# Sixty-two maxima instead of forty-eight between the q projections, and a new split of the x and q tiles in the first stage

## The chip, the cores and the metric

One Trainium2 chip, of which one core is used. The metric is the device time of one execution in microseconds (us); lower is better. The kernel before takes 1730.11 us, the median of three runs (1729.96, 1730.11 and 1730.19).

## The reference

The input `x` has 2048 rows (the sequence) and 640 columns. Two things are computed from it and mixed by a gate, all in float32:

```python
g = _sigmoid((x * gate_w).sum(-1, keepdims=True))
# A: real part of a Fourier transform along both axes, as matrix products
a = x @ dft_hid_re.T ; b = x @ dft_hid_im.T
y = dft_seq_re @ a - dft_seq_im @ b
# B: attention with 32 heads of 20 columns that share one k and one v
q = (x @ wq) ; k = x @ wk ; v = x @ wv            # q: 32 heads x 20
p = softmax(q_h @ k.T * 20 ** -0.5) ; o_h = p @ v
out = g * y + (1 - g) * (concat(o_h) @ wo)
```

The softmax needs the maximum of each row of scores. This kernel computes the scores twice: once only for the maxima ("a" matmuls, each followed by a maximum on VectorE), and a second time, with the maximum already in the contraction, for the exponential ("b" matmuls).

## The kernel before, in words

**Number format.** A float32 product is made of three products of rounded parts: each operand is split into a high part (rounded, tagged float32r) and the low rest, and `mm3` adds high x high, high x low and low x high in PSUM. A split is one copy on ScalarE (the high part) and one subtraction on VectorE (the low part); weights and later tiles are split on GpSimd.

**Stages.** The program runs in four parts.

1. *The q stage.* The sequence is cut in four blocks of 512 columns (ROW); the contraction over 640 is cut in five chunks of 128. For each block n there is a `kv` product of 10 matmuls (k, v and the gate together), four small transposes `kvt`, and five q projections (m = 0 to 4) of 15 matmuls each. `q_out` reads a finished projection from PSUM, splits it into the tiles `qh` and `ql`, and stores both to DRAM (`qh_d`, `ql_d`). `load_qs0` and `load_qs` read rows of one head pair back into `qs`, in the layout that the scores need. `kv_out` writes k into the tile `ks` by six small moves per block.
2. *Between the projections,* from block 1 on, some of the maxima of head pair 0 are computed: `a_half` issues one score matmul of 60 rows and 512 columns on TensorE and one `tensor_reduce` on VectorE that takes its maximum. The table `slots` says after which projections, and four calls are made each time, into the PSUM banks S1, S2, S3 and S4. Before the change that is 2 x 4 in block 1, and 5 x 4 in each of blocks 2 and 3: 48.
3. *The lead stage.* The first 8 groups of the Fourier part (`ab`, 120 steps of two matmuls with 64 rows and 320 columns each) run with further maxima between them, until 2 x (32 + 12) = 88 maxima are done in all: 40 in this stage before the change. The banks of these maxima are S2, S3 and S4 in turn; the groups of `ab` use S0 with F0 and S1 with F1, in turn.
4. *The loop,* and then a tail, which hold most of the time: the rest of the Fourier part, maxima, exponentials and their products with v, by hand-written plans. The change touches none of it.

**What sets the order.** On TensorE, ScalarE, VectorE and GpSimd the instructions stand in the order of the code. All moves go through one queue on SyncE (SP in the profile), and that queue is ordered by the framework's scheduler, not by the code: it may put a load ahead of moves that stand earlier in the code. SP issues strictly one after the other: a move that waits holds up all behind it.

**Tiles and banks that the change touches.** `xr` holds a block of x (five chunks) until it is split, with two buffers; `qh` and `ql` have three buffers each, and each is free again when its store to DRAM has landed. The eight PSUM banks are S0 to S4, F0, F1 and V; in blocks 1 to 3 the banks F1, V, S0 and F0 are handed out in turn to `kv`, `kvt` and the q projections. Two buffers named raw (`raw_tile`) are shared by parts of `wq`, the weights of the Fourier part (`load_w`, loaded as two parts and split on GpSimd by `split_w`), and the first tiles of x for the lead stage (`load_x`, the loads `xraw` that the first `ab` groups read).

Of the kernel before, what the change touches and what calls it, by code (L numbers as in the profile page):

```python
# [8 lines left out]
F32 = mybir.dt.float32  # L9
F32R = mybir.dt.float32r  # L10
AF = mybir.ActivationFunctionType
ALU = mybir.AluOpType
# [5 lines left out]
P = 128  # L18
S = 2048
# [3 lines left out]
KC = D // P  # L23
# [6 lines left out]
ROW = 512  # L30
# [3 lines left out]
def kernel(  # L34
# [13 lines left out]
    nc = tc.nc  # L48
# [64 lines left out]
    def move(dst, src):  # L113
        nc.sync.dma_start(words(dst), words(src))  # L114
# [22 lines left out]
    xT_v = xT.rearrange("(c p) t -> p c t", p=P)  # L137
# [167 lines left out]
    def a_half(hh, tag="A"):  # L305
        u = state[hh]
        if u >= NA:
            return
        a_unit(u, hh, tag)
        if steps:  # L310
            f, v = steps.pop(0)
            f(v)
        state[hh] = u + 1
        if state[1 - hh] <= u:
            return
        v, r = divmod(u, UV)
        if r == 8 and v + 1 < 2 * NPAIR:
            load_qs(v + 1)
        if r == UV - 1:
            steps.extend((f, v) for f in (a_reduce, a_turn, a_high, a_final))  # L320
            if not stage["loop"]:
                do_chores()
# [24 lines left out]
    with ExitStack() as c1:  # L347
        w1 = c1.enter_context(tc.tile_pool(name="w1", bufs=1, side="right"))
        x1 = c1.enter_context(tc.tile_pool(name="x1", bufs=2, side="right"))
        rot = Rot(["S1", "S0", "F0", "S2", "S3", "S4", "F1", "V", "S0", "F0"])  # L350
        kvg = w1.tile([P, KC, 41], F32, name="kvg")
        kvgs = w1.tile([P, KC, P], F32R, name="kvgs")
        nc.gpsimd.memset(kvgs.bitcast(F32), 0.0)
        nc.gpsimd.memset(ks.bitcast(F32), 1.0)
        nc.gpsimd.memset(vsb, 1.0)
        wqh = w1.tile([P, KC, D], F32R, name="wqh")
        wql = w1.tile([P, KC, D], F32R, name="wql")
        wq_v = wq.rearrange("(c p) n -> p c n", p=P)
        xs, xsp = {}, {}

        def load_x1(n, c):
            if n < 4:
                if c == 0:
                    xs[n] = x1.tile([P, KC, ROW], F32, name="xr")
                move(xs[n][:, c], xT_v[:, c, n * ROW : (n + 1) * ROW])

        def split_x1(n, c):
            if n < 4:
                if c == 0:
                    xh = x1.tile([P, KC, ROW], F32R, name="xh")  # L370
                    xl = x1.tile([P, KC, ROW], F32R, name="xl")
                    xsp[n] = (xh, xl)
                xh, xl = xsp[n]
                nc.scalar.activation(xh[:, c], xs[n][:, c], AF.Copy)
                nc.vector.tensor_tensor(xl[:, c], xs[n][:, c], xh[:, c].bitcast(F32), op=ALU.subtract)

        def q_mm(ps, n, m, c):
            ms = slice(m * P, (m + 1) * P)
            xh, xl = xsp[n]
            mm3(ps, wqh[:, c, ms], wql[:, c, ms], xh[:, c], xl[:, c], KC, c)  # L380

        def q_out(ps, n, m):
            ms, ts = slice(m * P, (m + 1) * P), slice(n * ROW, (n + 1) * ROW)
            qh = x1.tile([P, ROW], F32R, name="qh", bufs=3)
            ql = x1.tile([P, ROW], F32R, name="ql", bufs=3)
            nc.scalar.activation(qh, ps, AF.Copy)
            nc.vector.tensor_tensor(ql, ps, qh.bitcast(F32), op=ALU.subtract)
            move(qh_d[ms, ts], qh)
            move(ql_d[ms, ts], ql)

        def kv_mm(ps, n, c):
            xh, xl = xsp[n]
            end = c == KC - 1
            for high in (not end, end):
                m, x = (105, xh) if high else (41, xl)
                nc.tensor.matmul(ps[:m], kvgs[:, c, :m], x[:, c], start=(c == 0 and high), stop=(end and high))

        def kv_out(ps, n):
            ts = slice(n * ROW, (n + 1) * ROW)
            kvT = x1.tile([41, ROW], F32, name="kvT")  # L400
            kvl = x1.tile([41, ROW], F32, name="kvl", bufs=1)
            kh = x1.tile([DH, ROW], F32R, name="kh")
            kl = x1.tile([DH, ROW], F32R, name="kl")
            nc.scalar.activation(kvl, ps[64:105], AF.Copy)
            nc.vector.tensor_tensor(kvT, ps[:41], kvl, op=ALU.add)
            nc.scalar.activation(kh, kvT[:DH], AF.Copy)
            nc.vector.tensor_tensor(kl, kvT[:DH], kh.bitcast(F32), op=ALU.subtract)
            for r0 in (0, 64):
                move(ks[r0 : r0 + 20, ts], kh)
                move(ks[r0 + 20 : r0 + 40, ts], kl)  # L410
                move(ks[r0 + 40 : r0 + 60, ts], kh)
            return kvT

        def kv_turn(kvT, n, rot):
            ps = rot(f"kvt_{n}")
            for j in range(4):
                nc.tensor.transpose(
                    ps[:, 64 * j : 64 * j + 41], kvT[:, j * P : (j + 1) * P], ident[:41, :41]
                )
            pv = ps.rearrange("p (j c) -> p j c", c=64)[:, :4]  # L420
            ns = slice(4 * n, 4 * n + 4)
            nc.scalar.activation(vsb[:, ns, :DH], pv[:, :, DH : 2 * DH], AF.Copy)
            nc.vector.tensor_copy(
                gz[:, ns].rearrange("p (j o) -> p j o", o=1), pv[:, :, 2 * DH : 2 * DH + 1]
            )


        def gate_out():
            nc.vector.tensor_scalar_max(gz, gz, -87.0)
            nc.scalar.activation(omg, gz, AF.Exp, scale=-1.0)  # L430
            nc.vector.tensor_scalar_add(omg, omg, 1.0)
            nc.vector.reciprocal(gate, omg)
            nc.vector.tensor_scalar(omg, gate, -1.0, 1.0, op0=ALU.mult, op1=ALU.add)

        load_x1(0, 0)
        move(kvg, wkvg.rearrange("(c p) n -> p c n", p=P))
        pkv = rot("kv_0")
        pq = [rot(f"q_0_{m}") for m in range(KC)]
        for c in range(KC):
            if c:  # L440
                load_x1(0, c)
            raw = raw_tile([P, D], "wraw") if c in (2, 3) else w1.tile([P, D], F32, name="wraw", bufs=2)
            move(raw, wq_v[:, c])
            if c == 0:
                nc.vector.tensor_copy(kvgs[:, :, :41], kvg)
                nc.vector.tensor_tensor(
                    kvgs[:, :, 64:105], kvg, kvgs[:, :, :41].bitcast(F32), op=ALU.subtract
                )
            split_x1(0, c)
            split(raw, wqh[:, c], wql[:, c])  # L450
            kv_mm(pkv, 0, c)
            for m in range(KC):
                q_mm(pq[m], 0, m, c)
        for c in range(KC):
            load_x1(1, c)
        for c in range(KC):
            split_x1(1, c)
        kvT = kv_out(pkv, 0)
        for m in range(KC):
            q_out(pq[m], 0, m)  # L460
        load_qs0(0)
        rot = Rot(["F1", "V", "S0", "F0"])
        slots = {1: (2, 3), 2: range(KC), 3: range(KC)}
        for n in range(1, 4):
            for c in range(KC):
                load_x1(n + 1, c)
            pkv = rot(f"kv_{n}")
            for c in range(KC):
                kv_mm(pkv, n, c)
            kv_turn(kvT, n - 1, rot)  # L470
            kvT = kv_out(pkv, n)
            if n == 3:
                for k in range(2):
                    load_x(k)
            for m in range(KC):
                ps = rot(f"q_{n}_{m}")
                for c in range(KC):
                    q_mm(ps, n, m, c)
                split_x1(n + 1, m)
                q_out(ps, n, m)  # L480
                if (n, m) == (1, 0):
                    load_qs0(1)
                if m in slots[n]:
                    for z in range(4):
                        a_half(z % 2, f"S{1 + z}")
                if (n, m) == (3, 1):
                    kv_turn(kvT, 3, rot)
                    gate_out()
                if n == 3 and m in (2, 3):
                    split_x(m - 2)  # L490
                if (n, m) == (3, 3):
                    load_x(2)
            if n < 3:
                load_w(n - 1, 0)
                split_w(n - 1)
# [102 lines left out]
    op = ctx.enter_context(tc.tile_pool(name="op", bufs=2))  # L598
# [605 lines left out]
```

## Time and profile before

| What | us |
|---|---|
| Median of the three runs | 1730.11 |
| The profiled execution, its time | 1732.34 |
| The profiled execution, span of its instructions | 1730.6 |
| q stage: first matmul of a `kv` product to the last of the last projection | 6.0 to 102.4 |
| Lead stage: first `ab` matmul to the first `b` matmul | 102.9 to 130.4 |
| Loop and tail | 130.4 to 1730.6 |

The profile is one execution, taken by the hardware. Its page gives busy times and a chain of work that ended last; the timeline, read for one engine or for all, gives the start and the length of each instruction, what its engine waited for before it (in brackets, with the releaser), and how many instructions were merged in the row (x). PE is TensorE, DVE is VectorE, ACT is ScalarE, POOL is GpSimd, SPq is the queue that issues the moves. A row of the windows view gives, for a stretch of time, the busy us of PE, PE's weight loads, DVE, ACT and POOL, each with its count of instructions, then the granted TensorE clock as a share of full speed, the share of DMA time and GB/s.

### The profile page before, as it was taken

The numbers are of one execution on the slowest core, as the hardware profiler recorded it, in microseconds if no ns is written. First come the engines' busy times: TensorE is split into PE (matmuls) and PEld (weight loads), VectorE is DVE, ScalarE is ACT, GpSimd is POOL, SyncE is SP. The second block draws the span as 40 slices with busy tenths as digits, with TensorE's granted clock in tenths as the row PEclk, the third lists the DMA queues.
The fourth block names the chain that finished last, engine by engine and source line by source line (L and its number), as shares of the span: only waits on it lengthen the run. The fifth ranks groups of instructions, "written<-read, shape, count | busy, mean of one in ns | idle before, by whom it ended". The sixth has DMA issues, their size and how long they took to land.

```text
span 1730.6 us, 43337 instructions
## 1 busy us (share of the span) xinstructions
PE 1710.9 (99%) x16752; PEld 1239.4 (72%) x16752; DVE 1381.5 (80%) x2290; ACT 1251.2 (72%) x2543; POOL 1104.3 (64%) x921
## 2 busy tenths in 40 slices
PE   8999999999999999999999999999999999999997
PEld 6686777777677777777777777777777777777664
DVE  5787888888888888888888888888888888888813
ACT  4237888888777677777777777777777767678895
POOL 3045556333356658758777887888877764557785
PEclk9999999999999999999999999999999999999999
DMA  8551223222175556545666776655555533143332
GB/s 270 155 168 56 71 79 105 82 73 72 61 227 168 174 169 196 170 156 200 223 215 211 231 236 217 205 187 185 177 173 170 155 112 111 57 127 117 100 100 85
DMA packets 181499, 261.47 MB, mean 151 GB/s; under 512 B 35696, under 2 KB 136304, under 8 KB 181292
## 3 DMA queue, kind: packets, MB, share of 16 engines
q1 hardware_dynamic: 181292, 258.70, 47.2%
q8 instruction: 132, 2.16, 0.5%
q14 instruction: 75, 0.61, 0.1%
HBM read 184.42 MB, written 76.99 MB: 151 GB/s over the span
## 4 chain that ended last, share of the span: by engine, by line
PE 93%; DMA 2%; DVE 2%; issue 1%; ACT 1%; SPq 1%; POOL 0%; POOLq 0%; DVEq 0%; ACTq 0%
PE av L974 27%; PE y_p L782 21%; PE b L962 18%; PE a L251 15%; PE ab L782 7%; PE oo L782 3%; DVE mx L258 1%; PE q L122 1%; PE q L123 1%; SPq L114 1%; PE q L124 1%; ACT pt L970 1%; DMA wraw<-in_wiT_dram 0%; DMA ql_d<-ql 0%; DMA wraw<-in_wq_dram 0%
## 5 line engine op out<-in xcount | busy, mean ns | idle before, releaser
L258 DVE TENSOR_REDUCE mx<-a 128x1 f32<-128x512 f32 x2048 | 1303.2, 686 | 246.6 <-PE a L251 197.4
L970 ACT ACTIVATE pt<-b 128x512 f32<-128x512 f32 x2048 | 1058.2, 623 | 342.8 <-PE a L251 262.3
L962 PE MATMUL b<-qs,ks 62*128 62x512 f32 x2048 | 755.4, 408 | 3.1 <-ACT pt L970 2.1
L251 PE MATMUL a<-ks,qs 60*128 60x512 f32 x2048 | 707.7, 408 | 2.2 <-DVE mx L258 2.2
L782 PE MATMUL y_p<-tb,ch 64*128 64x320 f32 x3584 | 618.6, 307 | 0.0
L782 PEld LDWEIGHTS y_p<-tb,ch 64*128 64x128 f32 x3584 | 504.3, 186 | 2.9
L974 PE MATMUL av<-pt,vsb 128*32 128x512 f32 x4096 | 485.8, 598 | 0.0
L962 PEld LDWEIGHTS b<-qs,ks 62*128 62x128 f32 x2048 | 345.5, 185 | 187.7 <-DVE mx L258 125.1
L782 PE MATMUL y_p<-tb,cl 64*128 64x320 f32 x1792 | 454.8, 306 | 0.0
L251 PEld LDWEIGHTS a<-ks,qs 60*128 60x128 f32 x2048 | 345.6, 185 | 16.0 <-issue 4.0
L782 PEld LDWEIGHTS y_p<-tb,cl 64*128 64x128 f32 x1792 | 297.2, 186 | 2.7
L974 PEld LDWEIGHTS av<-pt,vsb 128*32 128x32 f32 x4096 | 111.5, 109 | 239.6 <-issue 229.9
L543 POOL TENSOR_TENSOR cl<-craw,ch 128x1024 fp32r<-128x1024 f32 x112 | 268.5, 2397 | 9.0
L824 POOL TENSOR_TENSOR yt<-yt,yu 128x320 f32<-128x320 f32 x86 | 75.0, 872 | 285.3 <-ACT yu L819 232.2
L824 POOL TENSOR_TENSOR abt<-abt,abu 128x320 f32<-128x320 f32 x64 | 55.8, 872 | 198.0 <-ACT abu L819 183.9
L537 POOL TENSOR_TENSOR craw<-craw 128x1024 f32<-128x1024 f32 x64 | 153.4, 2397 | 0.0
L542 POOL CAST ch<-craw 128x1024 fp32r<-128x1024 f32 x112 | 116.6, 1041 | 13.5 <-DMA craw<-in_cre_dram 6.9
L782 PE MATMUL oo<-wo,osp 64*128 64x320 f32 x816 | 91.5, 307 | 0.0
L782 PEld LDWEIGHTS oo<-wo,osp 64*128 64x128 f32 x816 | 86.6, 185 | 1.5
L569 POOL TENSOR_TENSOR tb<-braw,tb 128x320 fp32r<-128x320 f32 x80 | 69.9, 880 | 0.0
L782 PE MATMUL ab<-wbh,xh 64*128 64x320 f32 x256 | 60.1, 306 | 0.0
L782 PE MATMUL ab<-wbh,xl 64*128 64x320 f32 x256 | 59.9, 306 | 0.0
(138 smaller groups left out, 1622.8 us busy)
## 6 DMA issues: line engine op xcount, KB each, us to landing
craw<-in_cre_dram SPq DMA_DIRECT2D x80, 512.0 KB
craw<-in_cim_dram SPq DMA_DIRECT2D x64, 512.0 KB
s_d<-craw SPq DMA_DIRECT2D x32, 512.0 KB
craw<-s_d SPq DMA_DIRECT2D x32, 512.0 KB
braw<-b_d SPq DMA_DIRECT2D x80, 160.0 KB
xraw<-in_xT_dram SPq DMA_DIRECT2D x32, 320.0 KB
b_d<-abt SPq DMA_DIRECT2D x64, 160.0 KB
t_d<-braw SPq DMA_DIRECT2D x64, 160.0 KB
```

The lines of the kernel that those rows point to most:

```text
L114: nc.sync.dma_start(words(dst), words(src))
L251: nc.tensor.matmul(ps, qs[v][b : b + 60, qb * P : (qb + 1) * P], ks[b : b + 60, c * ROW : (c + 1) * ROW], start=True, stop=True,)
L258: nc.vector.tensor_reduce(mx[v][:, hh, qb, c : c + 1], ps, axis=AX.X, op=ALU.max)
L537: nc.gpsimd.tensor_tensor(x, raw[0], x, op=how)
L542: nc.gpsimd.tensor_copy(h, x)
L543: nc.gpsimd.tensor_tensor(l, x, h.bitcast(F32), op=ALU.subtract)
L569: nc.gpsimd.tensor_tensor(t[:, 1], raw, t[:, 0].bitcast(F32), op=ALU.subtract)
L782: nc.tensor.matmul(ps, w, x, start=start, stop=stop)
L824: nc.gpsimd.tensor_tensor(t0, t0, t1, op=ALU.add)
L962: nc.tensor.matmul(ps, ks[b : b + 62, kc * P : (kc + 1) * P], qs[NPAIR * (qc // 2) + p][b : b + 62, (qc % 2) * ROW : (qc % 2 + 1) * ROW], ...
L970: nc.scalar.activation(t, ps, AF.Exp, scale=SCALE)
L974: nc.tensor.matmul(ps[32 * g : 32 * g + 32, :], vsb[:, kc, :], t, start=first, stop=last)
```

## The change

The change has four edits, all in the q stage.

- `slots` becomes the number of calls after each projection: 0, 0, 4, 4, 4 in block 1, five times 4 in block 2 and five times 6 in block 3, which are 12 + 20 + 30 = 62. The lead stage then has 26, since the sum of 88 stays.
- The calls use the banks S1, S2, S3, S4 and F0 in turn, starting at S1 after each projection; F0 is taken out of the banks that the projections use.
- The x of the first block is loaded into five tiles that share the buffers of `qh` (tag "qh"); blocks 1 to 3 share one `xr` buffer instead of two.
- `qh` and `ql` have five buffers each instead of three.

```diff
         def load_x1(n, c):
             if n < 4:
-                if c == 0:
-                    xs[n] = x1.tile([P, KC, ROW], F32, name="xr")
-                move(xs[n][:, c], xT_v[:, c, n * ROW : (n + 1) * ROW])
+                if n == 0:
+                    xs[n, c] = x1.tile([P, ROW], F32, tag="qh", name="xr0", bufs=5)
+                else:
+                    if c == 0:
+                        xs[n] = x1.tile([P, KC, ROW], F32, name="xr", bufs=1)
+                    xs[n, c] = xs[n][:, c]
+                move(xs[n, c], xT_v[:, c, n * ROW : (n + 1) * ROW])
...
-            qh = x1.tile([P, ROW], F32R, name="qh", bufs=3)
-            ql = x1.tile([P, ROW], F32R, name="ql", bufs=3)
+            qh = x1.tile([P, ROW], F32R, tag="qh", name="qh", bufs=5)
+            ql = x1.tile([P, ROW], F32R, name="ql", bufs=5)
...
-        rot = Rot(["F1", "V", "S0", "F0"])
-        slots = {1: (2, 3), 2: range(KC), 3: range(KC)}
+        rot = Rot(["F1", "V", "S0"])
+        slots = {1: (0, 0, 4, 4, 4), 2: (4, 4, 4, 4, 4), 3: (6, 6, 6, 6, 6)}
...
-                if m in slots[n]:
-                    for z in range(4):
-                        a_half(z % 2, f"S{1 + z}")
+                for z in range(slots[n][m]):
+                    a_half(z % 2, ("S1", "S2", "S3", "S4", "F0")[z % 5])
```

What this does to the order of the instructions shows at three places.

**SP's queue near the start,** before the change. `wrT` and `wiT` are the weights of the Fourier part in two parts each; `xr` are the loads of x for the q stage, and the ten in one row are those of blocks 2 and 3; `ks` and `qh_d` are the first moves that the maxima need:

```order
L114 DMA wraw<-in_wrT_dram 128x3x320
L114 DMA wraw<-in_wrT_dram 128x2x320
L114 DMA xr<-in_xT_dram 128x512 x10
L114 DMA wraw<-in_wiT_dram 128x3x320
L114 DMA wraw<-in_wiT_dram 128x2x320
L114 DMA ks<-kh 20x512
```

The same place after the change:

```order
L114 DMA wraw<-in_wrT_dram 128x3x320
L114 DMA wraw<-in_wrT_dram 128x2x320
L114 DMA wraw<-in_wiT_dram 128x3x320
L114 DMA xr<-in_xT_dram 128x512 x5
L114 DMA wraw<-in_wiT_dram 128x2x320
L114 DMA xraw<-in_xT_dram 128x5x128 x2
L114 DMA ks<-kh 20x512
```

Only block 2 of x is loaded here now (block 3 comes after the last stores of block 1). One part of `wiT` has moved ahead of it, and the two `xraw` loads of the lead stage, which stood behind the `ks` moves of block 3 before, now stand ahead of the first `ks` move. The first `xraw` load goes into the buffer of the first part of `wiT`, the second into that of the second part.

**TensorE's queue in block 3,** before the change, from the last matmul of projection 0 to the first of projection 1 (`a_14_0` is unit 14 of the maxima for the first head of the pair, `a_14_1` for the second):

```order
L124 MATMUL q_3_0_825<-xh_601,wql_143 128x512
L251 MATMUL a_14_0_847<-ks_98,qs0_117 128x512
L251 MATMUL a_14_1_850<-ks_98,qs0_117 128x512
L251 MATMUL a_15_0_853<-ks_98,qs0_117 128x512
L251 MATMUL a_15_1_856<-ks_98,qs0_117 128x512
L122 MATMUL q_3_1_859<-xh_601,wqh_142 128x512
```

After the change:

```order
L124 MATMUL q_3_0_841<-xh_617,wql_143 128x512
L251 MATMUL a_16_0_863<-ks_98,qs0_117 128x512
L251 MATMUL a_16_1_866<-ks_98,qs0_117 128x512
L251 MATMUL a_17_0_869<-ks_98,qs0_117 128x512
L251 MATMUL a_17_1_872<-ks_98,qs0_117 128x512
L251 MATMUL a_18_0_875<-ks_98,qs0_117 128x512
L251 MATMUL a_18_1_878<-ks_98,qs0_117 128x512
L122 MATMUL q_3_1_881<-xh_617,wqh_142 128x512
```

The first five of a group go to S1, S2, S3, S4 and F0, and the sixth (here `a_18_1`) to S1 again, the bank of the first (`a_16_0`).

**TensorE's queue at the start of the lead stage,** after the change (the last two maxima of the q stage, and the first `ab` matmuls, whose names end in the half of the group: `ab_0_0` is in S0, `ab_0_1` in F0):

```order
L251 MATMUL a_30_0_1055<-ks_98,qs0_117 128x512
L251 MATMUL a_30_1_1058<-ks_98,qs0_117 128x512
L785 MATMUL ab_0_0_1075<-w0h_551,xh_833 128x320
L785 MATMUL ab_0_1_1076<-w0h_551,xh_833 128x320
L785 MATMUL ab_0_0_1075<-w0h_551,xl_834 128x320
```

`a_30_0` is the fifth of its group and stands in F0, which the second matmul of the lead stage writes. Before the change F0 held a projection here and no maximum.

More of the change, by code (lines that the diff above doesn't have):

```diff
@@ L373, in split_x1 @@
                 xh, xl = xsp[n]
-                nc.scalar.activation(xh[:, c], xs[n][:, c], AF.Copy)
-                nc.vector.tensor_tensor(xl[:, c], xs[n][:, c], xh[:, c].bitcast(F32), op=ALU.subtract)
+                nc.scalar.activation(xh[:, c], xs[n, c], AF.Copy)
+                nc.vector.tensor_tensor(xl[:, c], xs[n, c], xh[:, c].bitcast(F32), op=ALU.subtract)
         def q_mm(ps, n, m, c):
```

## The prediction

> **What bounds the kernel now.** I read the page first, then the clock and the busy times by windows, then the timeline of the first 140 us, since the change touches nothing behind it.
>
> ```profile
> span 1730.6 us, 43337 instructions
> PE 1710.9 (99%) x16752; PEld 1239.4 (72%) x16752; DVE 1381.5 (80%) x2290; ACT 1251.2 (72%) x2543; POOL 1104.3 (64%) x921
> PE 93%; DMA 2%; DVE 2%; issue 1%; ACT 1%; SPq 1%; POOL 0%; POOLq 0%; DVEq 0%; ACTq 0%
> ...
> 40.00:41.00 1.00, 1.00 (x4) 0.81 (x3) 0.98 (x2) 0.97 (x2) 0.00 (x0) 0.50 1.02 205
> 80.00:100.00 20.00, 20.00 (x94) 14.15 (x93) 14.16 (x28) 5.56 (x11) 2.11 (x2) 1.00 0.54 162
> 100.00:120.00 20.00, 17.76 (x183) 16.42 (x183) 18.53 (x35) 5.99 (x14) 10.06 (x10) 1.00 0.51 161
> ```
>
> TensorE holds 93% of the chain, so a wait moves the end only if TensorE stands for it, and a shift at the loop's start arrives at the end nearly whole: the loop is TensorE's too. In the q stage (80 to 100) PE is busy for all 20 us and DVE for 14.2; in the lead stage (100 to 120) DVE has 18.5 of 20 and PE 17.8. So the maxima are taken from a stage where VectorE is nearly full and put into one where it has room. That speaks for the change. Whether it pays is decided by what TensorE, which issues in order, then waits for.
>
> ```profile
> 34.86 0.60 ACT L386 ACTIVATE qh<-q 128x512 fp32r<-128x512 f32 x1 [8.06 <-DMA qh_d<-qh]
> 39.47 0.56 PE L122 MATMUL q<-xh,wqh 128*128 128x512 f32 x1 [2.92 <-DVE kvT L405]
> 43.20 0.39 PE L122 MATMUL q<-xh,wqh 128*128 128x512 f32 x1
> 44.68 0.80 PE L251 MATMUL a<-ks,qs 60*128 60x512 f32 x4
> ```
>
> The other wait that the change aims at is here. ScalarE waits 8.06 us for a `qh` buffer, `kv_out` behind it is late, and TensorE stands 2.92 us for the bank. Then the clock is 0.50 (row 40 to 41): the nine matmuls from 39.47 to 43.20 take 3.73 us, where nine at 0.233 (14 steps between the rows 98.67 and 102.04 below, less their slow first one) would take 2.1. So 1.6 us go there. The first maxima start at 44.68.
>
> **The q tiles.** Five buffers end ScalarE's wait, so TensorE comes to the end of projection 2 of block 1 at about 39.47 − 2.92 + 15 × 0.233 = 40.1. But the four maxima that stand next in its queue need `ks` and `qs`, which come over SP.
>
> ```profile
> 11.16 1.87 SPq L114 DMA_DIRECT2D wraw<-in_wrT_dram  x2
> 13.26 11.04 SPq L114 DMA_DIRECT2D xr<-in_xT_dram  x10
> 24.39 0.91 SPq L114 DMA_DIRECT2D wraw<-in_wiT_dram  x2
> 25.40 0.91 SPq L114 DMA_DIRECT2D ks<-kh  x1
> 32.19 0.36 SPq L114 DMA_DIRECT2D qh_d<-qh  x1
> 42.35 0.27 SPq L114 DMA_DIRECT2D qs<-ql_d  x1
> 83.41 0.77 SPq L114 DMA_DIRECT2D ks<-kh  x1
> 88.18 0.99 SPq L114 DMA_DIRECT2D xraw<-in_xT_dram  x2
> ...
> 16.09 5.95 DVE L375 TENSOR_TENSOR xl<-xr,xh 128x512 fp32r<-128x512 f32 x5
> ...
> 8.76 5.80 DMA wraw<-in_wq_dram
> ...
> 17.34 1.50 POOL L211 CAST w0h<-wraw 128x960 fp32r<-128x960 f32 x1 [12.43 <-DMA wraw<-in_wrT_dram]
> 22.70 1.57 POOL L212 TENSOR_TENSOR wbl<-wraw,wbh 128x640 fp32r<-128x640 f32 x1
> 32.18 0.99 POOL L211 CAST w1h<-wraw 128x960 fp32r<-128x960 f32 x1 [7.90 <-DMA wraw<-in_wiT_dram]
> 35.44 0.72 POOL L211 CAST wbh<-wraw 128x640 fp32r<-128x640 f32 x1
> 36.24 1.54 POOL L212 TENSOR_TENSOR wbl<-wraw,wbh 128x640 fp32r<-128x640 f32 x1
> ```
>
> Before, the `ks` moves follow `wiT` at once (25.40). After, two `xraw` loads stand between, and the second needs the buffer of the second part of `wiT`, which is free when GpSimd has split that part. I follow this chain. Block 2's x waits for VectorE's five `xl` (16.09 + 5.95 = 22.04) and is issued by about 24.3, as the second five were before (13.26 + 11.04 = 24.30); the second `wiT` part needs the `wbl` that ends at 24.27 and follows. It lies behind 1.3 MB of x, as `wrT` did (11.16 to 17.34, 6.2 us) and `wiT` (24.39 to 32.18, 7.8 us); a part of `wq` of the same size among the first loads took 5.80. I take 6.2: 30.5. GpSimd splits it in 36.24 + 1.54 − 35.44 = 2.3, so `xraw` goes at 32.9, and half a pair's 0.99 later, at 33.4, the six `ks` moves start. Where nothing delays them they take 88.18 − 83.41 = 4.8, so the first store of q is issued at 38.2 instead of 32.19: **6.0 us later**. From that store to the first maxima the way was 44.68 − 32.19 = 12.5, of which I take 1.2 off for stores that ScalarE's wait held back. So the first maxima start at about 49.5, **+4.8**, and TensorE stands from 40.1 to 49.5 in one piece. By 5.80 and 7.8 for the load and 11 to 12.5 for the way it is 48.6 to 52; if the load hardly waits for x, 47. The slow clock comes behind it again: the 1.6 us that were ahead of 44.68 are now behind 49.5, **+1.6**, between 0 (a clock that comes back while the maxima wait for VectorE) and 3.2 (twice as long). What is hidden: the single `xr` buffer. Block 3's x now goes after block 1's stores, but its splits start only after the first projection of block 2, and five loads need about 2.5 us.
>
> **The maxima that are moved.** One more group of four stands in block 1 (after projection 4), and two more in each group of block 3.
>
> ```profile
> 97.68 0.40 PE L124 MATMUL q<-xh,wql 128*128 128x512 f32 x1
> 98.01 0.73 PE L251 MATMUL a<-ks,qs 60*128 60x512 f32 x4
> 98.16 0.60 ACT L386 ACTIVATE qh<-q 128x512 fp32r<-128x512 f32 x1 [3.13 <-issue]
> 98.67 0.50 PE L122 MATMUL q<-xh,wqh 128*128 128x512 f32 x1
> 98.79 0.69 DVE L387 TENSOR_TENSOR ql<-q,qh 128x512 fp32r<-128x512 f32 x1 [1.27 <-ACT qh L386]
> 99.40 2.47 DVE L258 TENSOR_REDUCE mx<-a 128x1 f32<-128x512 f32 x4
> 102.04 0.40 PE L124 MATMUL q<-xh,wql 128*128 128x512 f32 x1
> ```
>
> Between the last matmul of a projection and the first of the next lie 98.67 − 97.68 = 0.99, where 0.233 would do: a group of four costs TensorE **0.8**. Its reading of `qs` for queries 512 to 1023 is fresh from DRAM there; I add **0.5** (0 to 2) for a wait.
>
> The groups of six cost more. The sixth matmul writes S1, so it waits until VectorE has taken the maximum of the first. And VectorE cannot start that early: ScalarE copies the projection (98.16), then comes `ql` (98.79), then the first maximum at 99.40. With 0.68 for one (2.47 less three steps of 0.60) it ends at 100.08, where before the next projection started at 98.67. The sixth matmul starts at about 100.1 and the projection 0.4 later, at 100.5 (the fourth of a group of four lies about as far ahead of it): **+1.8 each**. Queued behind the waiting matmul are the next 15 matmuls, for whose projection ScalarE and VectorE then wait in turn, so nothing makes it up. Four such gaps lie between projections: **+7.3**. The fifth is the lead's start. Without the wait for S1, two more would cost 0.15 to 0.2 each, and the four gaps about +1.4: the low end of this term.
>
> **The lead stage.**
>
> ```profile
> 103.77 12.04 DVE L258 TENSOR_REDUCE mx<-a 128x1 f32<-128x512 f32 x20
> 105.10 0.49 PE L251 MATMUL a<-ks,qs 60*128 60x512 f32 x1 [1.55 <-DVE mx L258]
> 110.51 0.47 PE L251 MATMUL a<-ks,qs 60*128 60x512 f32 x1
> 111.10 0.47 PE L251 MATMUL a<-ks,qs 60*128 60x512 f32 x1
> 117.48 0.50 PE L251 MATMUL a<-ks,qs 60*128 60x512 f32 x1 [0.69 <-DVE mx L258]
> 134.26 0.31 PE L782 MATMUL ab<-wbh,xh 64*128 64x320 f32 x2
> 134.41 0.31 PE L782 MATMUL ab<-wbh,xl 64*128 64x320 f32 x2
> ```
>
> VectorE takes 20 maxima in 12.04, 0.60 each, without a gap, and looks like the bound. But TensorE needs as long: from maximum to maximum 0.59 (110.51, 111.10) with three steps of `ab` between, and a step without any takes 0.15 (134.26, 134.41), so three steps and a maximum are four slots of 0.15. Fourteen fewer free 14 × 0.15 = 2.1 us of TensorE, not 14 × 0.60 = 8.4 of VectorE; with the wait of 0.69 that is −2.8. At its start the stage loses: its second matmul needs F0, where the fifth maximum of the last group stands. That ends 99.40 − 97.68 + 4 × 0.60 + 0.68 = 4.8 us after the last matmul of the projection; before, TensorE was held until 105.10 − 102.04 = 3.1. So +1.7, in all **−1.1**. Ends: −2.8, and +1 if moves that are now counted by fewer maxima hold a tile.
>
> **The sum:** 4.8 + 1.6 + 0.8 + 0.5 + 7.3 − 1.1 = +13.9. The profiled execution took 1732.34 (span 1730.6), so 1746.2 on its scale; the median of the runs is 2.2 below it, so I predict 1730.1 + 13.9 = **1744.0**.
>
> **A rule against the change.** In block 3 TensorE would stand 1.8 us in every 6.2. Before, the wait up to 105.10 of similar length left the clock at 1.00 (row 100 to 120); after the one of 2.92 us it was 0.50. I take it that the clock stays up. The Trainium skill, "TensorE: Matmul & The Clock Gate", section "A second HAM failure mode: psum-queue depth-cycling", says that TensorE idling briefly between groups as banks are cycled can make the clock swing between half and full. By that rule the time would be the one of the clock rival below; its section "What's actually happening" puts the fall after an idle window of about 3.4 us, and here 2.92 was enough, so the trace decides.
>
> **The rivals.**
> - *The load queue does not hold* (9%): the second `wiT` part lands and is split so early that the maxima start by 44.7. For it: the load is ordered after half as much x as before. Against it: the rows 6.2 and 7.8, and six `ks` moves that cannot start earlier than before. Without 4.8 and 0.5: +8.6, 1738.7.
> - *Faster: the maxima are free between the projections* (6%). The q tiles end the wait at 39.47 and VectorE has room for the rest. The place is the sixth matmul: if the first maximum were done when it is issued (about 0.9 after the last matmul of the projection, not 2.4), the groups would cost 0.15 a maximum, and F0 would be free at the lead's start. With the first maxima at 40.1 (−4.6) the sum is −4.6 + 0.8 + 1.4 − 2.8 = −5.2: 1724.9. It needs the load queue to be early too. Against it: the chain 98.16, 98.79, 99.40 is in the order of each engine.
> - *The sixth maximum waits little, the load queue holds* (4%): 13.9 − 7.3 + 1.4 = +8.0, 1738.1.
> - *The clock falls in block 3* (4%): 75 matmuls at twice 0.233 add up to 17: 1761.
> - *Both costs small, gains and losses cancel* (4%): 1728 to 1732.
>
> **The chances.** The forecast has 73%. About 0.2%, 3.5 us, is what a measurement of this kernel tells from no change; beyond it slower gets 73 + 9 + 4 + 4 = 90%, the same 4%, faster 6%. The range takes in the ends of the load queue's delay and the two small-cost rivals on the slow side, and leaves out the clock, the cancelling and the faster case: 1735 to 1752.
>
> **What would show it.** Right: in the profile after, SP's first `ks` move near 33 and behind two `xraw` rows; a wait of TensorE of 7 to 12 us before the first maxima of block 1, near 49.5, and a clock of 0.50 behind it; projections of block 3 that follow each other in 6.2 us instead of 4.36, with a wait of TensorE for `mx` before the last maximum of each group; a wait for `mx` at the second `ab` matmul; and a lead stage of about 27 us. Wrong: first maxima before 45; gaps in block 3 below 1.5 us; or a loop that starts later by the sum and ends by less, which would mean that something in it makes up for lost time.

## The result and the profile after

| | Before | After |
|---|---|---|
| Median of four runs each, us | 1730.15 | 1749.21 (1747.30 to 1751.93) |
| Ratio, with its 95% interval | | 1.0106 [1.0085, 1.0126] |
| Profiled execution: time and span, us | 1732.34, 1730.6 | 1751.93, 1750.1 |

The change makes the kernel 19 us slower; 1744.0 was predicted. The two profiled executions differ by 19.5 us of span, so they can be compared piece by piece. First the head of the page after, and then, of the view that sums up waits, TensorE's three longest rows for the first 160 us (engine, operation and line, releaser: us in total, how many, the longest):

```profile
span 1750.1 us, 43343 instructions
PE 94%; DMA 2%; issue 1%; DVE 1%; ACT 1%; SPq 1%; POOL 0%; POOLq 0%; ACTq 0%; DVEq 0%
```

```profile
PE a L251 <- DMA qs<-ql_d: 12.5, 1, 12.5
PE a L251 <- DVE mx L258: 5.8, 5, 1.2
PE ab L785 <- DVE mx L258: 1.9, 1, 1.9
```

TensorE still holds the chain, and its new waits are the three that the prediction names: one for the first maxima, five for a sixth maximum, one at the lead's start. They add up to 20.2 us; a wait of 2.92 is gone.

**The front.** SP's queue, then GpSimd's, then TensorE's first groups of maxima, in the timeline of after:

```profile
21.45 0.37 SPq L114 DMA_DIRECT2D wraw<-in_wiT_dram  x1
23.13 2.24 SPq L114 DMA_DIRECT2D xr<-in_xT_dram  x5
25.46 0.57 SPq L114 DMA_DIRECT2D wraw<-in_wiT_dram  x1
29.06 6.51 SPq L114 DMA_DIRECT2D xraw<-in_xT_dram  x2
35.67 0.91 SPq L114 DMA_DIRECT2D ks<-kh  x1
40.58 0.42 SPq L114 DMA_DIRECT2D qh_d<-qh  x1
...
32.81 0.72 POOL L211 CAST wbh<-wraw 128x640 fp32r<-128x640 f32 x1 [3.78 <-DMA wraw<-in_wiT_dram]
33.61 1.57 POOL L212 TENSOR_TENSOR wbl<-wraw,wbh 128x640 fp32r<-128x640 f32 x1
...
52.52 1.70 PE L251 MATMUL a<-ks,qs 60*128 60x512 f32 x4 [12.55 <-DMA qs<-ql_d]
59.79 0.73 PE L251 MATMUL a<-ks,qs 60*128 60x512 f32 x4
71.35 0.74 PE L251 MATMUL a<-ks,qs 60*128 60x512 f32 x4
```

The second `xraw` load goes out when GpSimd's `wbl` ends (33.61 + 1.57 = 35.18), and the first `ks` move follows at 35.67, where it went out at 25.40 before. The first maxima start at 52.52 instead of 44.68. Between them and the second group lies one projection, which takes 7.27 us (59.79 less 52.52) instead of 4.43 (49.11 less 44.68 in the timeline of before). The clock (the number ahead of the last two, in the windows view of after) shows why:

```profile
48.00:52.00 4.00, 0.00 (x0) 0.00 (x0) 0.69 (x1) 0.23 (x1) 0.00 (x0) 0.50 0.80 199
52.00:56.00 4.00, 3.48 (x8) 2.27 (x9) 2.68 (x5) 0.00 (x0) 0.00 (x0) 0.50 0.21 52
56.00:60.00 4.00, 4.00 (x14) 2.94 (x14) 0.40 (x1) 0.05 (x1) 0.00 (x0) 0.69 0.71 213
100.00:104.00 4.00, 4.00 (x13) 2.88 (x14) 1.05 (x2) 0.05 (x1) 0.00 (x0) 0.64 0.41 140
104.00:108.00 4.00, 2.84 (x17) 2.00 (x16) 3.42 (x6) 0.78 (x2) 0.00 (x0) 1.00 0.49 165
```

**Block 3.** Its five groups of maxima on TensorE in after, the first six maxima on VectorE, and the lead's first wait:

```profile
95.99 0.96 PE L251 MATMUL a<-ks,qs 60*128 60x512 f32 x5
98.12 0.50 PE L251 MATMUL a<-ks,qs 60*128 60x512 f32 x1 [1.16 <-DVE mx L258]
103.79 0.96 PE L251 MATMUL a<-ks,qs 60*128 60x512 f32 x5
110.03 0.96 PE L251 MATMUL a<-ks,qs 60*128 60x512 f32 x5
112.16 0.50 PE L251 MATMUL a<-ks,qs 60*128 60x512 f32 x1 [1.17 <-DVE mx L258]
117.84 0.96 PE L251 MATMUL a<-ks,qs 60*128 60x512 f32 x5
124.09 0.96 PE L251 MATMUL a<-ks,qs 60*128 60x512 f32 x5
...
97.39 3.67 DVE L258 TENSOR_REDUCE mx<-a 128x1 f32<-128x512 f32 x6
...
128.61 0.41 PE L785 MATMUL ab<-w0h,xh 64*128 64x320 f32 x1 [1.89 <-DVE mx L258]
```

VectorE starts the first maximum 1.40 us after the group (95.99 to 97.39); it ends 0.68 later, at 98.07, and the sixth matmul starts at 98.12. From group to group it is 7.80, 6.24, 7.81 and 6.25 us, where it was 4.36 before. The stalls are alike to 0.01 us; in two of the four the clock has also fallen (0.64 in the row 100 to 104), which costs 1.56 more each.

**Where the 19.5 us are.** Four marks cut a span: the first group of maxima in block 2, the first and the last in block 3, and ScalarE's first `pt` (the loop's first exponential: 130.88 before, 152.07 after). The table gives the stretches between them for every kernel of this study, each from its own profiled execution.

| us | start to block 2 | block 2 | block 3, to its last group | lead, to the first `pt` | first `pt` to the end |
|---|---|---|---|---|---|
| before | 60.10 | 24.63 | 17.64 | 28.51 | 1599.7 |
| after | 71.35 | 24.64 | 28.10 | 27.98 | 1598.0 |
| e1 tiles only | 70.24 | 25.25 | 17.64 | 28.62 | 1597.0 |
| e2 maxima only | 64.57 | 24.63 | 26.54 | 28.73 | 1597.5 |
| e3 xraw from ScalarE | 60.41 | 24.99 | 28.13 | 28.01 | 1596.0 |
| e4 fives | 70.30 | 26.96 | 18.59 | 28.01 | 1599.8 |
| e5 sixth later | 62.33 | 24.64 | 21.97 | 28.00 | 1595.8 |
| e6 fives, xraw from ScalarE | 59.90 | 26.95 | 18.59 | 28.00 | 1599.2 |
| e7 the same, F0 first | 63.03 | 25.77 | 18.57 | 24.72 | 1599.3 |
| e8 front late | 56.40 | 33.18 | 17.64 | 28.61 | 1599.7 |
| e9 and x of block 3 early | 56.34 | 28.89 | 17.66 | 28.61 | 1599.6 |
| e10 the same, fives | 54.87 | 27.91 | 18.57 | 26.87 | 1600.0 |

After less before: 11.25 + 0.01 + 10.46 − 0.53 − 1.7 = 19.5. So there are two costs of nearly equal size, the front and block 3, and the lead stage, from which 14 of 40 maxima were taken, is 0.5 us shorter.

### The profile page after: what moved, and what is told of

Its sections match the earlier page's. It is cut to its first block, busy times and chain, and to the rows that moved or that the text cites. A ratio compares the mean times of both kernels' runs of the same rounds, so it can differ in the third digit from the quotient of the medians.

```text
span 1750.1 us, 43343 instructions
## 1 busy us (share of the span) xinstructions
PE 1716.3 (98%) x16752; PEld 1242.6 (71%) x16752; DVE 1384.7 (79%) x2290; ACT 1251.4 (71%) x2543; POOL 1104.7 (63%) x921
## 4 chain that ended last, share of the span: by engine, by line
PE 94%; DMA 2%; issue 1%; DVE 1%; ACT 1%; SPq 1%; POOL 0%; POOLq 0%; ACTq 0%; DVEq 0%
PE av L977 27%; PE y_p L785 21%; PE b L965 18%; PE a L251 15%; PE ab L785 7%; PE oo L785 3%; PE q L122 1%; PE q L123 1%; PE q L124 1%; SPq L114 1%; DMA wraw<-in_wq_dram 1%; ACT pt L973 1%; DMA wraw<-in_wiT_dram 0%; PE kv L400 0%; DVE xl L379 0%
## 5 line engine op out<-in xcount | busy, mean ns | idle before, releaser
L343 POOL TENSOR_TENSOR xl<-xraw,xh 128x640 fp32r<-128x640 f32 x6 | 9.4, 1566 | 82.6 <-ACT xh L342 82.6
```

## The experiments

Differences from before are against the runs of the kernel before on the same chip (medians 1732.49 for e1 to e4, 1732.25 for e5 to e8, 1731.08 for e9 and e10).

**e1: the tiles alone.** After, with the maxima and banks of before:

```diff
-        rot = Rot(["F1", "V", "S0"])
-        slots = {1: (0, 0, 4, 4, 4), 2: (4, 4, 4, 4, 4), 3: (6, 6, 6, 6, 6)}
+        rot = Rot(["F1", "V", "S0", "F0"])
+        slots = {1: (2, 3), 2: range(KC), 3: range(KC)}
...
+                if m in slots[n]:
+                    for z in range(4):
+                        a_half(z % 2, f"S{1 + z}")
```

> The x and q tiles of the change with the 48 maxima and the banks of before. Nothing is left out. Theory (my prediction's load queue): the scheduler still puts the second wiT part and two xraw loads ahead of the first ks move, so the first maxima of block 1 start near 52 with a wait of TensorE of 11 to 13 us for the DMA of qs, and a slow clock behind it; block 3 stays at 4.4 us a projection; the time is 8 to 11 us above the kernel before, some 1739 to 1741. Rival (the maxima alone cost the time, the tiles are free or help): the first maxima start at 40 to 45 and the time is 1725 to 1731.

Measured: 1741.91 us, +9.4; ratio 1.0057 [1.0042, 1.0072]. TensorE in e1:

```profile
52.76 1.70 PE L251 MATMUL a<-ks,qs 60*128 60x512 f32 x4 [12.59 <-DMA qs<-ql_d]
70.24 0.73 PE L251 MATMUL a<-ks,qs 60*128 60x512 f32 x4
```

The front is that of after (70.24 against 71.35), and block 3 that of before, 17.64. The rival falls: the x and q tiles alone, with no maximum more, cost 9 us, and the wait that they bring has the place and length of the one in after. That it comes by SP's order of moves is what e3 tries; which of the two tile edits changes that order was not tried apart.

**e2: the maxima alone.** Before, with the change's `slots`, banks and `rot` (the last two edits of the diff) and the x and q tiles of before.

> The 62 maxima and the banks of the change with the x and q tiles of before. Nothing is left out. Theory (the sixth maximum of a group waits for the first, and the clock falls in half of these gaps): TensorE waits some 1.2 us for mx five times in block 3, projections there follow each other in 6.2 to 7.8 us, the first maxima of block 1 stand where they stood before; the time is 8 to 11 us above the kernel before, 1738 to 1741. Rival A (the clock falls only because the long wait of block 1 has shifted the stage against the clock's own windows): all gaps 6.2 us, the time 1736 to 1738. Rival B (the load queue is the whole cause): within 2 us of the kernel before.

Measured: 1744.60 us, +12.1; ratio 1.0074 [1.0057, 1.0091]. Block 3 is 8.9 us longer, with gaps of 6.24, 6.26, 7.79 and 6.25: the clock fell in one of the four. So the gaps of rival A, all at 6.2, did not come; but block 3 starts 4.5 us later here than before (89.20 against 84.73), so that a shift has to do with the clock is not excluded. The time is above the theory's 8 to 11 because the first maxima did not stay at 44.68. ScalarE and then TensorE in e2:

```profile
35.20 0.60 ACT L386 ACTIVATE qh<-q 128x512 fp32r<-128x512 f32 x1 [8.31 <-DMA qh_d<-qh]
...
39.90 0.76 PE L122 MATMUL q<-xh,wqh 128*128 128x512 f32 x1 [6.76 <-DVE kvT L405]
48.65 0.73 PE L251 MATMUL a<-ks,qs 60*128 60x512 f32 x4
```

ScalarE waits for a `qh` buffer as before (8.06 there). With three banks instead of four, it is a projection earlier that comes round to the bank of `kv` and waits for `kvT` (which VectorE makes from that product), so TensorE stands 6.76 us instead of 2.92. In the whole change the five q tiles hide this cost of the fourth bank: in e3, which has both, no wait for `kvT` is left.

**e3: the two xraw loads out of SP's queue.** After, with:

```diff
-            move(raw, xT_v[:, :, t * P : (t + 1) * P])
+            q = nc.scalar if k < 2 else nc.sync
+            q.dma_start(raw, xT_v[:, :, t * P : (t + 1) * P])
```

> The whole change, with the first two xraw loads issued by ScalarE's own queue, so that no load that waits for a buffer stands ahead of the first ks move. Nothing is left out. Theory (the two xraw loads are what delays the ks moves): the first ks move is issued right behind wiT, the first maxima of block 1 start between 42 and 46, the long wait of TensorE is gone or under 4 us; block 3 keeps its 10 us; the time is 8 to 11 us below the changed kernel, 1738 to 1741. Rival (the second wiT part itself, late behind x, is the delay, or the stores are): the first ks moves near 30 or later and under 4 us are won, 1745 to 1749.

Measured: 1739.99 us, 9.2 below after (+7.5 over before, where after has +19.1); ratio 1.0044 [1.0029, 1.0059]. SP, then TensorE, in e3:

```profile
24.29 0.39 SPq L114 DMA_DIRECT2D wraw<-in_wiT_dram  x1
25.27 0.90 SPq L114 DMA_DIRECT2D ks<-kh  x1
...
42.40 1.28 PE L251 MATMUL a<-ks,qs 60*128 60x512 f32 x4 [2.30 <-DMA qs<-ql_d]
60.41 0.74 PE L251 MATMUL a<-ks,qs 60*128 60x512 f32 x4
```

The first `ks` move goes out 10 us earlier, right behind `wiT`, and block 2 starts at 60.41 instead of 71.35. The second `wiT` part is still issued behind x, so that by itself isn't the delay: what costs is a load that waits for GpSimd's split, with the moves that TensorE needs behind it in one queue. Block 3 keeps its 28.13.

**e4: fives instead of sixes.** After, with the same 62 maxima:

```diff
-        slots = {1: (0, 0, 4, 4, 4), 2: (4, 4, 4, 4, 4), 3: (6, 6, 6, 6, 6)}
+        slots = {1: (0, 0, 4, 4, 4), 2: (5, 5, 5, 5, 5), 3: (5, 5, 5, 5, 5)}
```

> The whole change with the same 62 maxima, but five after each projection of blocks 2 and 3 (12 + 25 + 25) instead of four and six, so that no maximum needs a bank of its own group. Nothing is left out. Theory (the sixth maximum of a group is what stalls): no wait of TensorE for mx in blocks 2 and 3, projections of both blocks follow each other in about 4.5 us, the clock stays at 1.00 there; the front wait stays; the time is 9 to 11 us below the changed kernel, 1738 to 1741. Rival (VectorE is the limit of the stage, whichever bank is used): projections 5 us or more apart in both blocks, and under 5 us won.

Measured: 1745.23 us, 4.0 below after (+12.7 over before); ratio 1.0071 [1.0056, 1.0086]. TensorE in e4:

```profile
97.26 0.97 PE L251 MATMUL a<-ks,qs 60*128 60x512 f32 x5
101.85 0.96 PE L251 MATMUL a<-ks,qs 60*128 60x512 f32 x5
...
120.37 0.49 PE L787 MATMUL ab<-w0h,xh 64*128 64x320 f32 x1 [3.55 <-DVE mx L258]
```

In block 3 the theory holds: no wait for `mx`, 4.59 from group to group (one group apart, 4.82, behind which a `kvt` stands), 9.5 us won. The time was missed because 4.1 us are given back: block 2 takes 2.3 more, and the stretch from the first `pt` 1.8 more (see the last section). In block 2 there are five maxima instead of four in a group, and one group is slow at a full clock (1.00 all through the block):

```profile
74.89 2.15 PE L251 MATMUL a<-ks,qs 60*128 60x512 f32 x5
```

It takes 2.15 us instead of 0.96, since its matmuls go at the pace of the maxima of the group before, which VectorE has not finished. ScalarE had waited 2.57 us for block 3's x, and VectorE for ScalarE. So the theory does not hold all through block 2: these two groups are 5.77 apart. With a front that is 1.05 shorter that leaves 6.4 in the profiled execution, and 4.0 between the medians.

**e5: the sixth maximum later.** e3, with the sixth matmul of a group in block 3 issued after nine matmuls of the next projection (the last group keeps its six together):

```diff
                 for c in range(KC):
                     q_mm(ps, n, m, c)
+                    if c == 2 and late:
+                        a_half(*late.pop(0))
...
+                    if z == 5 and m < 4:
+                        late.append((z % 2, "S1"))
```

> The kernel of e3 (the whole change, the first two xraw loads from ScalarE's queue) with one more edit: in block 3 the sixth matmul of a group is issued after nine matmuls of the next projection instead of ahead of them; same 62 maxima, same banks. Nothing is left out. Theory (what costs is that the projection stands in line behind a matmul that waits): no wait for mx in the four gaps between projections of block 3, these follow each other in 4.8 us (4.36 plus two maxima at 0.23), the clock stays at 1.00 from 84 to 108, the last group starts about 9 us earlier than in e3, and the time is 7 to 9 us below e3, 1731 to 1733. Rival (VectorE or the banks limit the stage, wherever the sixth stands): the wait moves into the projection or to its bank, 5.5 us or more a projection, under 4 us won.

Measured: 1735.31 us, 4.7 below e3 (+3.1 over before); ratio 1.0020 [1.0011, 1.0030]. Around one late maximum on TensorE, in e5:

```profile
89.83 0.40 PE L124 MATMUL q<-xh,wql 128*128 128x512 f32 x1
90.16 0.50 PE L251 MATMUL a<-ks,qs 60*128 60x512 f32 x1
90.59 0.50 PE L122 MATMUL q<-xh,wqh 128*128 128x512 f32 x1
```

No sixth maximum between projections waits, and the clock stays at 1.00 in block 3, which takes 21.97 instead of 28.13. So the same 62 maxima in the same banks cost 6.2 us less by their place in TensorE's queue: the cost was that the projection stood in line behind a matmul that waits. The theory's 9 was too much: a single maximum among the matmuls of a projection costs 0.62, not 0.23 (the second matmul behind it starts at 90.92, and 90.92 − 89.83 less two steps of 0.233 is 0.62). With the 4.59 of a group of five (e4) that makes 5.21 from group to group, as measured; one gap kept a wait for `mx` of 0.85; and the front was 1.9 longer than e3's, with a wait for `qs` of 3.62.

**e6 and e7: both remedies, and the bank order.** e6 is e3 with e4's `slots`; e7 is e6 with the banks of a group in another order:

```diff
-                    a_half(made_a % 2, ("S1", "S2", "S3", "S4", "F0")[z])
+                    a_half(made_a % 2, ("F0", "S1", "S2", "S3", "S4")[z])
```

> The whole change with both remedies: the first two xraw loads from ScalarE's queue (e3) and 12 + 25 + 25 maxima instead of 12 + 20 + 30 (e4). Nothing is left out. Theory (the two costs are apart and add up): no long wait at the front, no wait for mx in blocks 2 and 3, 4.6 us a projection; the first lead matmul waits 3.5 us for the fifth maximum in F0; time 1730 to 1735, that is 14 to 19 below the changed kernel and about level with the kernel before. Rival (one covers the other, so that the second brings little): 1737 or more.

> The kernel of e6 with the banks of each group of five in the order F0, S1, S2, S3, S4, so that the maximum in F0 is the first of the last group and not its fifth. Nothing is left out. Theory (the wait at the start of the lead is the bank's): the wait of the first lead matmuls falls from 3.5 to about 1.2 us, the clock stays at 1.00 behind it, the lead stage gets 2 to 3 us shorter, and so does the time: 1728 to 1732. Rival (the lead stage is bound by VectorE's backlog, so the wait turns up at the first maximum of the lead instead): a new wait for mx there and less than 1 us won.

Measured: e6 1733.75 us, +1.5, ratio 1.0015 [1.0005, 1.0025]; e7 1732.06 us, −0.2, ratio 0.9999 [0.9989, 1.0008]. The two costs are apart, and e6 removes both, but for a wait for `qs` of 2.0 at the front and one slow group in block 2 (2.14 us) as in e4. The lead's first wait in e7:

```profile
109.50 0.41 PE L788 MATMUL ab<-w0h,xh 64*128 64x320 f32 x1 [1.16 <-DVE mx L258]
```

It falls from 3.55 to 1.16, the clock behind it stays at 1.00, and the lead stage takes 24.72 instead of 28.00. So the bank was the cause of that wait. Of the 3.3 us that the stage gains on e6 only 1.7 are left in the medians: e7's front is 3.1 longer, with a wait for `qs` of 3.81 and a slow clock behind it, and its block 2 is 1.2 shorter. Against before, 14 fewer maxima are worth 28.51 − 24.72 = 3.8 us to the lead once its start is clean. Between the projections the same 14 cost 2.9: 1.14 in block 2 (25.77 − 24.63), 0.93 in block 3 (18.57 − 17.64), and 0.87 for one more group of four in block 1 (4.36 from group to group, less 15 × 0.233). The move as such is worth about 0.9 us.

**e8: the front alone, and later.** The tiles of the change, e3's loads, the banks and the 48 maxima of before, but the first group one projection later:

```diff
-        slots = {1: (0, 0, 4, 4, 4), 2: (4, 4, 4, 4, 4), 3: (6, 6, 6, 6, 6)}
+        slots = {1: (0, 0, 0, 4, 4), 2: (4, 4, 4, 4, 4), 3: (4, 4, 4, 4, 4)}
```

> The x and q tiles of the change and the xraw loads from ScalarE's queue, but the 48 maxima and the banks of before, with the first group after projection 3 of block 1 instead of 2 (0, 0, 0, 4, 4, then four each). Nothing is left out. Theory (the only gain that is to be had here is the front wait): TensorE goes from projection 2 to 3 without a wait for qs or kvT, the clock stays at 1.00 there, block 1's first group of four starts near 44 and its second near 48 where they started at 44.7 and 49.1 with one projection less before them, so block 2 starts some 4 us earlier than in the kernel before; time 3 to 5 us below before, 1726 to 1729 beside 1730.1 to 1732.5. Rival (a wait elsewhere takes its place, for qs or in the lead): within 2 us of before.

Measured: 1736.70 us, +4.5; ratio 1.0014 [0.9981, 1.0048], too wide for a verdict, so the trace decides. SP, ScalarE and TensorE in e8:

```profile
57.00 2.80 SPq L114 DMA_DIRECT2D xr<-in_xT_dram  x5
...
63.57 0.63 ACT L379 ACTIVATE xh<-xr 128x512 fp32r<-128x512 f32 x1 [8.51 <-DMA xr<-in_xT_dram]
...
66.19 2.58 PE L251 MATMUL a<-ks,qs 60*128 60x512 f32 x4 [5.37 <-DVE mx L258]
```

Block 2 starts 3.7 us earlier than before, as the theory has it, and then a wait elsewhere, of the kind that the rival names, takes back more than all of it. The single `xr` buffer brings block 3's x behind block 1's last stores, at 57.00; ScalarE, which splits it between two projections of block 2, waits 8.51 us for it; VectorE and its maxima wait for ScalarE, and TensorE for them. Block 2 is 8.6 us longer, the slow clock behind the wait included (0.50 for 6.8 us from 64.7).

**e9 and e10: block 3's x from another queue.** e9 is e8 with

```diff
+                q = nc.gpsimd if n == 3 else nc.sync
+                q.dma_start(xs[n, c], xT_v[:, c, n * ROW : (n + 1) * ROW])
```

and e10 has also (0, 0, 0, 4, 4), then fives, with F0 first.

> The kernel of e8 with one more edit: the x of block 3, which waits for the single xr buffer, is loaded from GpSimd's queue instead of behind the last stores of block 1 in SP's. Nothing is left out. Theory (in e8 the single xr buffer took the place of the front wait): block 3's x is issued near 48 instead of 57.0, ScalarE's wait of 8.5 us for it goes, and with it TensorE's wait of 5.4 before the second group of block 2 and the slow clock behind it; block 2's first projections follow each other in 4.36; the loop starts 3 to 4 us earlier than in the kernel before; time 1727 to 1730 beside some 1732 for the kernel before, and 7 to 9 below e8. Rival (TensorE waits there for something else, the maxima or qs): the wait stays above 3 us and under 3 us are won on e8.

> The kernel of e9 with more maxima between the projections, without a sixth and with the bank F0 first: 8 + 25 + 25 = 58 instead of 48. Nothing is left out. Theory (a maximum costs TensorE 0.23 between projections and saves a slot of 0.15 and some of VectorE's backlog in the lead stage, so the move itself is worth next to nothing): within 1.5 us of e9, the lead stage 3 to 4 us shorter, blocks 2 and 3 some 2.3 us longer, and the front of block 2 as in e9. Rival (the move of maxima off the lead stage is worth what VectorE's 0.60 per maximum says, 6 us): 3 us or more below e9.

Measured: e9 1731.91 us, +0.8, ratio 1.0002 [0.9993, 1.0011]; e10 1730.36 us, −0.7, ratio 0.9998 [0.9989, 1.0006]. ScalarE's wait for `xr` is gone, and e9 lies some 3.6 nearer to before than e8, but the next wait stands in the same place, in e9:

```profile
59.06 0.70 PE L251 MATMUL a<-ks,qs 60*128 60x512 f32 x3 [2.26 <-DMA qs<-ql_d]
```

The rows of `qs` for queries 512 to 1023 are not there yet; with 0.75 ahead of the group's first matmul that makes 3.0 us, and the clock falls behind it. The 3.8 us at the start of block 2 are lost again (28.89 for the block). e10 lies 1.6 below e9, about as its theory has it, with a block 2 that starts 5.2 us earlier than before and is 3.3 longer; its lead stage is 1.7 shorter than e9's, not 3 to 4, as the clock fell at its start. No version tried is measurably faster than the kernel before.

## Why the prediction was right in its direction and 5 us short

The sum was +13.9 on the profiled execution and 19.5 was measured. Its steps:

| Step | Predicted | Measured | Shown by |
|---|---|---|---|
| First maxima later (load queue) | +4.8 | +7.84 | e1 has it, e3 removes it |
| Slow clock behind the wait | +1.6 | +2.84 | clock rows 48 to 60 |
| One more group in block 1, and `qs` | +1.3 | +0.57 | 11.25 − 7.84 − 2.84 |
| Sixth maximum, block 3 | +7.3 | +10.46 | e2 has it, e4 and e5 remove it |
| Lead stage | −1.1 | −0.53 | table; e7 for the bank |
| From the first `pt` | 0 | −1.7 | table |

- **The load queue.** The mechanism is shown: e1 and e3. The size was short because every link was taken too short, two of them at or near the lower of my bounds. The second `wiT` part reached GpSimd at 32.81 where I took 30.5; `ks` went out at 35.67 instead of 33.4, and the first store at 40.58 instead of 38.2; from there to the maxima it was 11.94 instead of 11.3. These make the missing 3.0. The wait, 12.55, lies beyond the 7 to 12 that I gave for it. The upper end of my bounds, 52, was the better value: the load did lie behind the x that was issued just ahead of it.
- **The clock at the front.** It lasted longer than I took it to: besides some ten matmuls of the projection, as before, the four maxima ahead of them ran at half speed too (1.70 us, 0.80 before).
- **The single `xr` buffer**, which the forecast takes as hidden, is hidden in after (block 2 takes 24.64, before 24.63), but not for good: with more maxima in block 2 a group there is 1.2 us slow behind it (e4, e6), and in e8, whose block 2 starts early, it costs 8.6 with the slow clock behind it. So that part holds for the front and the maxima of this change, and not for the tiles as such.
- **The wait for fresh `qs`**, 0.5, didn't come in block 1 of after. It came in e9, where everything else was early.
- **The sixth maximum.** Stall, releaser and place are as predicted, 1.8 to 1.9 each by gaps of 6.24. The step that failed is "I take it that the clock stays up": it fell in two of the four gaps, 2 × 1.56 = 3.1 us. My ground was one wait of 1.55 in the lead stage behind which it stayed at 1.00, and one case isn't a rule. The rule that I set against the change, the Trainium skill's "TensorE: Matmul & The Clock Gate", section "A second HAM failure mode: psum-queue depth-cycling", says that short pauses between groups as the banks are cycled make the clock go to and fro, and here the trace agrees with it, by half: five of the twelve such gaps of after, e2 and e3. The clock rival (1761, all of block 3 at half clock) was still further off than the forecast.
- **The lead stage.** The wait for F0 came (1.89), but 3.4 us behind it (130.15 to 133.56) ran at half clock, which I had not counted; where it didn't fall, in e7, the stage gained 3.8, more than my best end of 2.8.
- **The faster case** fell at both of its conditions. e3 and e6 show that even with the load queue mended it would not have come: 14 moved maxima are worth 0.9 us (e7).
- **From the first `pt`**, 1.7 us came back: the loop starts 21.2 later and ends 19.5 later, which is the last of the prediction's signs of being wrong. No step of the change explains it; the last section shows that the clock at the loop's start accounts for 1.6.

## What to carry to other kernels

When buffers change, read the order of the move queue again before any time is estimated: a load that waits for a buffer holds every move behind it, and here it cost as much as the visible part of the change. A matmul that waits costs the whole queue behind it, so put it behind work that is ready (e5), or give it a bank that is free (e4, e7). Price a moved piece at its new place as well as at its old one, each on the engine that bounds that stage: VectorE's 0.60 per maximum was never to be had, since TensorE paid 0.21 at the one place and saved 0.27 at the other (2.9 and 3.8, by 14).

## What the runs showed of the hardware that was not expected

**The clock doesn't follow from the length of a wait.** The stalls of block 3 are alike (1.16 to 1.18 us in after, e2 and e3), and the clock fell in five gaps of twelve. The loop's start, whose instructions are the same in before and in e1, shows it best: the same three waits in both, shifted by 10.9 us. The windows view of before, then of e1, each just behind the third of these waits:

```profile
137.43 0.49 PE L962 MATMUL b<-qs,ks 62*128 62x512 f32 x1 [0.66 <-ACT pt L970]
...
139.00:140.00 1.00, 1.00 (x9) 0.00 (x0) 0.00 (x0) 0.00 (x0) 0.92 (x3) 0.50 0.23 78
140.00:141.00 1.00, 1.00 (x6) 0.36 (x4) 0.00 (x0) 0.00 (x0) 1.00 (x2) 0.50 0.00 0
```

```profile
148.32 0.49 PE L966 MATMUL b<-qs,ks 62*128 62x512 f32 x1 [0.66 <-ACT pt L974]
...
150.00:151.00 1.00, 1.00 (x12) 0.36 (x6) 0.00 (x0) 0.00 (x0) 0.92 (x3) 1.00 0.45 158
151.00:152.00 1.00, 1.00 (x16) 1.00 (x14) 0.84 (x2) 0.87 (x2) 1.00 (x2) 1.00 0.00 0
```

In before the clock is 0.50 there, in e1 1.00. What it costs shows at the 21st `pt`, in ScalarE's rows of before and of e1:

```profile
148.03 2.07 ACT L970 ACTIVATE pt<-b 128x512 f32<-128x512 f32 x4 [0.83 <-PE b L962]
```

```profile
157.32 3.16 ACT L974 ACTIVATE pt<-b 128x512 f32<-128x512 f32 x6 [0.83 <-PE b L966]
```

From the first `pt` (130.88 and 141.75) that is 17.15 in before and 15.57 in e1, so the slow stretch costs 1.6 us; through the rest of the loop before stays 1.0 to 1.6 behind, and 1.6 at the last `pt`. The other 1.2 of the difference between 1599.7 and 1597.0 in the table arise in the tail, behind the last `pt`. In the table this stretch is 1599.2 to 1600.0 in the seven kernels whose clock fell at the loop's start, and 1595.8 to 1598.0 in the five where it didn't, among them after. The runs of one kernel are spread over 4.9 us here (1728.96 to 1733.82 in 26 of 27 runs of before, the other took 1749.73), so no step that is worth less than 2 us can be judged from a median of few.

**In these traces the clock changes only on a grid of 3.41 us.** In all twelve, each slow stretch between 20 and 170 us lasts 3.41 us or two, three or four times that, and where a trace has more than one, they begin whole multiples of 3.41 us apart. In after they begin at 44.81, 99.43, 113.08 and 130.15, which are 16, 4 and 5 steps. I take it that the clock is set by what lies in the step before, and then a shift moves the same waits to other places in the steps: e1's loop is 10.87 us later than before's, which is 3.18 steps. The Trainium skill, same page, section "What's actually happening", says that the clock follows activity in windows that run freely and don't start with the kernel, and the traces agree. It puts the fall after an idle window of some 3.4 us, and here it fell after waits of 0.66 and 1.2, so on that the measurement decides.

How much a step must hold to keep the clock up stays open. TensorE's busy time alone doesn't tell: in after it is 2.26 us in the step from 96.01, behind which the clock fell, and 2.26 in the step from 102.84, behind which it didn't. A kernel shifted by a known delay, and nothing else, was not tried.
